# The opening of an FFT-and-MLP kernel: input ahead of the weights, most scratch rows written late, weights prepared inside the first steps

## The chip, the core and the metric

The kernel runs on one NeuronCore of a Trainium2 chip. The metric is the device time of one execution in microseconds (us). The core has five engines, each with its own queue that is worked off in order: TensorE (PE, matrix products; PEld is its loading of weights), VectorE (DVE), ScalarE (ACT), GpSimd (POOL) and SyncE (SP, here only an issuer of transfers). Transfers are issued by SP and by GpSimd, and all of them share the same 16 DMA engines.

## What is computed

A two-dimensional Fourier transform over sequence and channels, of which the real part is kept, and then a two-layer MLP with the hard-swish activation:

```python
X = np.fft.fft(x, axis=1)          # x: (8, 3008, 256)
X = np.fft.fft(X, axis=2).real
x = X.reshape(24064, 256)
h = x @ w_in                       # (256, 2048), float64 in memory
g = h * np.clip(h + 3.0, 0.0, 6.0) / 6.0
out = g @ w_out                    # (2048, 256), float64 in memory
```

## The kernel before

**Stages.** The eight sequences are worked in four pairs. The transform over 3008 = 47 x 64 positions has two stages. For stage 1, x is loaded in eight chunks per pair (`load_x`, L136: the rows themselves, L146, and their mirrored partners by an indirect transfer, L155, whose indices `IX` come with the constants `F`). A fold (`fold`, L160, five additions and subtractions) makes sums and differences of rows and mirrored rows; one matmul of 512 columns per half chunk with `F` (`stage1`, L214, L227) follows, and `evict_z` (L230) copies the result to the tile z and writes it to a scratch tensor `zd` in DRAM. Column 128 needs another treatment: `turn_column` (L251) writes it, with signs changed, to a second scratch tensor `zq` in 4-byte elements. `load_g` (L261) reads the scratch back, turned, in six groups per pair; `stage2` (L271, L284) multiplies a group with a table `T`, and `spread` (L290) spreads one row of its result over all partitions (`qn`). The transform over channels is not done at all: it is folded into w_in (`fold_w_in`, L566), which makes `W1`; one row of W1 is kept in another layout as `WN`, by way of DRAM (L580, `load_wn`).

**Main loop.** The MLP runs in 12 chunks per pair and 8 steps per chunk, 384 steps in all (`steps`, L742). In step s, `mlp1` (L324) is issued for step s + 2: four first-layer matmuls of 256 columns into two PSUM tiles u and v (L334), two operations on VectorE that add the row WN (L339), a sum and a difference (L349, L351), two relus on ScalarE (L376) and two gates on VectorE (L379) that give the tile a with four blocks. `combine` (L381) makes sums of these blocks on GpSimd (L393). `mlp2` (L395) multiplies seven blocks (Strassen's scheme in Winograd's form: seven products in place of eight) with seven combinations `G` of w_out (L403) and accumulates over the 8 steps; `finish` (L413) puts the seven results together on GpSimd, and `store` turns and writes them. A matmul in 32-bit floats shows as two records in the trace.

**Weights.** w_in and w_out come as 64-bit floats and are turned into 32-bit ones by hand, in 16 pieces of 512 KB (`PIECES`, L480; `load_w`, L485, issued by GpSimd). A piece takes, on ScalarE, the two parts of `exponent_a` (L509) and `exponent_c` (L518); on TensorE, `exponent_b` (L514, two matmuls that subtract 16-bit numbers); on VectorE, `mantissa` (L526, L527) and `join` (L535 or L542). Two finished pieces of w_in go to `fold_w_in` (L574, copies to W1 on ScalarE, L579), two of w_out to `mix_w_out` (L556), which makes the combinations G on VectorE (L561 to L564).

**Order.** The order on each engine is the program's order. In the opening, the loop over the chunks of pair 0 (L658) takes one chunk of x and one weight piece together; these chunks use shorter functions (`fold_first`, L184, three VectorE operations, and `stage1_first`, L194, four matmuls per half chunk) save the last one. Then come the load of g for group 0 and seven more pieces (L677), each with a filler product (`keep_awake`, L594) for TensorE's clock; after that stage 2 and `spread` of group 0 and the first two `mlp1`. The last piece is finished after step 1 (`after`, L698). What is done beside the steps of a pair (further stage-2 groups, and loading, folding and stage 1 of the next pair, nine steps per chunk, the fold on GpSimd) stands in `beside` (L700) with step numbers.

Of the kernel before, what the change touches and what calls it, by code (L numbers as in the profile page):

```python
# [51 lines left out]

PROD = ("P1", "P2", "-P4", "P5", "P7", "-P6", "P3")
# [3 lines left out]
def kernel(  # L57
# [51 lines left out]
    F = consts.tile([PR + 2, 5 * PZ + NP * NXC + 1], F32, name="F")  # L109
# [17 lines left out]
    def x_tile(pr, i):  # L127
        pool, tag = xpool, "x"
        if pr.p == 0 and 4 <= i < 13:
            pool, tag = ((apool, "a"), (cpool, "c"), (spool, "t"))[(i >= 8) + (i >= 11)]  # L130
        return pool.tile([PR + 2, XC, D], F32, tag=tag, name="xt")
# [8 lines left out]
    def load_forward(pr, c):  # L140
        xt = x_tile(pr, 2 * c)

        nr = PR + 2 if pr.p < NP - 1 else PR
        rows = x_pn[pr.p * PR:pr.p * PR + nr]
        n = XC if c < NXC - 1 else XC - 1
        nc.gpsimd.dma_start(out=xt[0:nr, 0:n, :], in_=rows[:, c * XC + 1:c * XC + 1 + n, :])  # L146
        if n < XC:
            nc.gpsimd.dma_start(out=xt[0:nr, n:XC, :], in_=rows[:, 0:1, :])
        pr.x[c] = xt

    def load_partners(pr, c):
        xr = x_tile(pr, 2 * c + 1)
# [31 lines left out]
    def fold_first(pr, c):  # L184
        xt, xr = pr.x[c][0:PR], pr.xr[c][0:PR]
        r = xr[:, ::-1, :]
        y = ypool.tile([PR, XC + 1, D], F32, tag="y", name="y")
        tt = nc.vector.tensor_tensor
        tt(y[:, 0:XC, 1:P], xt[:, :, D - 1:P:-1], r[:, :, 1:P], op=AL.add)
        tt(xt[:, :, 1:P], xt[:, :, 1:P], r[:, :, D - 1:P:-1], op=AL.add)  # L190
        tt(xt[:, :, 0:P + 1:P], xt[:, :, 0:P + 1:P], r[:, :, 0:P + 1:P], op=AL.add)
        pr.y[c] = y

    def stage1_first(pr, c, i):  # L194
        sl = slice(2 * i, 2 * i + 2)
        a, b = pr.x[c][0:PR, sl, :], pr.y[c][:, sl, 1:P]
        ps = bank([P, 2, D], "ps1")
        for k, (f, m, c0) in enumerate([(F[0:PR, 0:PZ], a[:, :, 0:P + 1], 0), (F[0:PR, 0:PZ], b, 1),
                                        (F[0:PR, 0:PZ], a[:, :, 1:P], P + 1), (FN[0:PR], b, P + 1)]):
            nc.tensor.matmul(ps[0:PZ, :, c0:c0 + m.shape[2]], f, m, start=(k == 0), stop=(k > 0),  # L200
                             skip_group_check=True)
        evict_z(pr, c, i, ps)
        if i == XC // 2 - 1:
            del pr.x[c], pr.xr[c]
# [9 lines left out]
    def stage1(pr, c, i):  # L214

        y = pr.y[c]
        ps = bank([P, 2, D], "ps1")
# [10 lines left out]
        evict_z(pr, c, i, ps)  # L228

    def evict_z(pr, c, i, ps):  # L230
        if i == 0:

            pool, tag = (gpool, "g") if pr.p == 0 and c % 3 == 2 else (zpool, "z")
            pr.z[c] = pool.tile([PZ, XC, D], F32, tag=tag, name="z")
            if c == 0:
                pr.zd = dpool.tile([2, NK1, 2, NS, D], F32, tag="zd", name="zd")
                pr.zq = dpool.tile([2, NK1, 2, NS], F32, tag="zq", name="zq")
        z = pr.z[c]
        nc.scalar.copy(z[:, 2 * i:2 * i + 2, :], ps[0:PZ])  # L239
        if i == XC // 2 - 1:  # L240
            nc.sync.dma_start(
                out=pr.zd[:].rearrange("b k c n d -> (b k c) n d")[:, c * XC:(c + 1) * XC, :],
                in_=z[:],
            )
            turn_column(pr, c, z)
            del pr.y[c], pr.z[c]

# [3 lines left out]
    def turn_column(pr, c, z):  # L251
        n = XC if c < NXC - 1 else XC - 1
        zc = zpool.tile([PZ, XC], F32, tag="zc", bufs=4, name="zc")
        nc.scalar.activation(zc[:, 0:n], z[:, 0:n, P], AF.Identity, scale=F[0:PZ, 5 * PZ + NP * NXC:])
        cs = slice(c * XC, c * XC + n)
        nc.sync.dma_start(out=pr.zq[:, :, ::-1, cs].rearrange("b k c n -> (b k) c n"), in_=zc[:, 0:n])
        if n < XC:
            nc.sync.dma_start(out=pr.zq[:, :, :, c * XC + n].rearrange("b k c -> (b k c)"), in_=z[:, n, P])


    def load_g(pr, gr):  # L261
        g = gpool.tile([P, 2 * KK, D + 1], F32, tag="g", name="g")
        ks = slice(gr * 2 * KK, (gr + 1) * 2 * KK)
        gb = [g[b * N2:(b + 1) * N2] for b in range(2)]
        for b in range(2):
            nc.sync.dma_start(out=gb[b][:, :, 0:D], in_=pr.zd[b].rearrange("k c n d -> (c n) k d")[:, ks, :])
        for b in range(2):
            nc.sync.dma_start(out=gb[b][:, :, D], in_=pr.zq[b].rearrange("k c n -> (c n) k")[:, ks])
# [36 lines left out]
    class Chunk:  # L305
# [3 lines left out]
        def __init__(self, pr, ck):  # L309
            self.pr, self.ck = pr, ck  # L310
            self.last = ck == NCK - 1
            self.final = self.last and pr.p == NP - 1
# [81 lines left out]

    def mlp2(ch, fc):  # L395
# [78 lines left out]
    FN = wpool.tile([PR + 2, PZ], F32, tag="FN", name="FN")  # L474
# [8 lines left out]
    raw, exs, fracs, w = {}, {}, {}, {}  # L483

    def load_w(j):  # L485
        kind, n, i = PIECES[j]
        st = wpool.tile([P, 2 * WB], I32, tag="st", bufs=4, name="st")
# [17 lines left out]
    def exponent_a(j):  # L505
        top = raw[j][:].bitcast(I16).rearrange("p (n four) -> p n four", four=4)[:, :, 3]
        for i in range(2):
            low = PM[:, j % 2, i].bitcast(U8).rearrange("p (n two) -> p n two", two=2)[:, :, 0]
            nc.scalar.activation(low, top, AF.Identity, bias=bias[:, i:i + 1], scale=(1 - 2 * i) / 16.0)  # L509

    def exponent_b(j):
        ex = ps_h.tile([P, WB], F32, tag="uv", name="ex")
        for i in range(2):
            nc.tensor.matmul(ex[:], E[:, i], PM[:, j % 2, i].bitcast(F16), start=(i == 0), stop=(i == 1))  # L514
        exs[j] = ex
# [4 lines left out]
    def mantissa(j):  # L520
# [3 lines left out]
        top = wpool.tile([P, WB], I32, tag="top", bufs=2, name="top")  # L524
# [5 lines left out]
    def join(j):  # L530
# [8 lines left out]
        b12 = wpool.tile([P, 2, P], F32, tag="b12", bufs=2, name="b12")[:] if i == 0 else None  # L539
        for h, g in enumerate((block(n, 0), b12) if i == 0 else (block(n, 1), block(n, 6))):  # L540
            f, e = (t.rearrange("p (c q h e) -> h p c q e", c=2, h=2, e=DH)[h] for t in (frac, ex))
            nc.vector.tensor_tensor(g.rearrange("p c (q e) -> p c q e", e=DH), f, e, op=AL.mult)  # L542
        if i == 0:
            w[PIECES[j]] = b12
# [4 lines left out]
    def use_pair(j):  # L549
        kind, n, _ = PIECES[2 * j]  # L550
        if kind == "in":
            fold_w_in(n)
        else:
            mix_w_out(n)

    def mix_w_out(j):  # L556

        b12 = w.pop(("out", j, 0))
        g = [block(j, i) for i in range(7)]
        tt = nc.vector.tensor_tensor  # L560
        tt(g[3], g[0], b12, op=AL.subtract)  # L561
        tt(g[5], g[6], g[3], op=AL.add)
        tt(g[2], g[5], g[1], op=AL.subtract)
        tt(g[4], g[6], b12, op=AL.subtract)  # L564

    def fold_w_in(n):  # L566

        cs = slice(n * WB, (n + 1) * WB)
        ws = [w.pop(("in", n, i)) for i in range(2)]
        sums = []  # L570
        for blk in range(2):
            ps = bank([P, WB], "wps")
            for i in range(2):
                nc.tensor.matmul(ps[:], C[:, i, blk * P:(blk + 1) * P], ws[i], start=(i == 0), stop=(i == 1))  # L574
            sums.append(ps)

        def copy():
            for blk in range(2):
                nc.scalar.copy(W1[:, blk, cs], sums[blk][:])  # L579
            nc.sync.dma_start(out=wn[n:n + 1], in_=W1[P - 1:P, 1, cs])  # L580

        copies.append(copy)


    def load_wn(n):
        nb = WB // P
        nc.sync.dma_start(out=WN[:, n * nb:(n + 1) * nb], in_=wn[n].rearrange("(j p) -> p j", p=P))
# [6 lines left out]
    def keep_awake(n):  # L594
        ps = ps_h.tile([P, 2 * TB], F32, tag="uv", name="awake")
        for i in range(n):
            nc.tensor.matmul(ps[:], ones[:], Z[:], start=True, stop=True)  # L597
# [4 lines left out]
    keep_awake(6)  # L602
    nc.sync.dma_start(out=F[:], in_=c_stage1)
# [4 lines left out]
    PM = wpool.tile([P, 2, 2, WB], I16, tag="PM", name="PM")  # L608
    nc.vector.memset(PM[:].rearrange("p j i n -> p (j i n)").bitcast(I32), 0x64006400)
    nc.vector.tensor_copy(IX[:], F[:, 5 * PZ:5 * PZ + NP * NXC])  # L610
    nc.scalar.mul(FN[:], F[:, 0:PZ], -1.0)
# [3 lines left out]
    nc.sync.dma_start(out=C[:], in_=dim[:, :, 0:D])  # L615
    E = wpool.tile([P, 2, P], F16, tag="E", name="E")
    nc.scalar.copy(E[:], CE[:])
    for b in range(2):
# [3 lines left out]
    wn = dpool.tile([NWI, WB], F32, tag="wn", bufs=1, name="wn")  # L622


    load_forward(first, 0)
    load_partners(first, 0)
    load_w(0)
    load_x(first, 1)
    load_w(1)
# [3 lines left out]
    pending, copies = [], []  # L633

    def on_scalar(j):
        for i in pending:
            exponent_c(i)
        if j is not None:
            exponent_a(j)
# [3 lines left out]
    def on_vector(j):  # L643
        if j is not None:
            mantissa(j)
        for i in pending:
            join(i)

    def on_tensor(j):
        if j is not None:  # L650
            exponent_b(j)
        done = pending.pop() if pending else 0
        if done % 2:
            use_pair(done // 2)
        if j is not None:
            pending.append(j)

    for c in range(NXC):  # L658
        if c + 2 < NXC:
            load_x(first, c + 2)  # L660
        load_w(c + 2)
        if c < NXC - 1:
            fold_first(first, c)
        else:
            for part in range(2):
                fold(first, c, part, nc.vector)
        on_scalar(c)
        on_vector(c)
        for i in range(XC // 2):
# [181 lines left out]
```

## Time and profile before

| | us |
|---|---|
| median of 3 runs (lowest, highest) | 1979.77 (1979.23, 1982.34) |
| the profiled execution, its time | 1980.04 |
| its span in the profile | 1978.3 |
| first stage-2 matmul (L284) | 77.4 |
| first second-layer product (L403), step 0 | 92.06 |
| TensorE busy in 0 to 100 us | 86.57 |
| TensorE busy in 300 to 400 us | 100.00 |
| ScalarE busy in 0 to 100 us | 60.08 |
| VectorE busy in 0 to 100 us | 59.99 |

In the profile, L12 means line 12 of the kernel before. A row of a group gives line, engine and operation, the tiles written and read, shapes and count, then busy time and the mean of one in nanoseconds, and then how long the engine stood idle ahead of these instructions and for whom. A row of waits gives who waited for whom: total, how often, longest. The chain of waits goes back from the last instruction, at each step to what released it; its rows are start, duration, what. PEclk, and the clock column of the stretches, is the TensorE clock granted, as a part of full speed.

### The profile page before, as it was taken

The page shows a single profiled execution, that of the slowest core. Times are in us where ns is not written, and L with a number is a line of the kernel's source. Part 1 is how long each engine was busy: PE and PEld are TensorE (multiplying, and loading weights), DVE is VectorE, ACT ScalarE, POOL GpSimd, SP SyncE. Part 2 cuts the span into 40 slices and gives each one's busy share as a digit, 9 for nine tenths or more (in the row PEclk, how much of TensorE's full clock was granted, in tenths as well). Part 3 has the DMA queues.
Part 4 walks back from the last instruction along what each step waited for, and adds up shares of the span by engine and source line. Part 5 has one row for each costly group of instructions (what it writes and reads, how often), then busy time and mean ns, then how long its engine had stood idle before and what let it go on. Part 6 is the DMA issues. An engine that isn't in the chain of part 4 may idle for free.

```text
span 1978.3 us, 27746 instructions
## 1 busy us (share of the span) xinstructions
PE 1949.1 (99%) x9178; PEld 1685.4 (85%) x9178; DVE 1433.5 (72%) x2775; ACT 687.9 (35%) x1164; POOL 1414.2 (71%) x1604
## 2 busy tenths in 40 slices
PE   8899999999999999999999999999999999999998
PEld 5588888888998888888898888888889888888887
DVE  5677767776787776776777776777678777777776
ACT  6533333333333333333333333333333333333332
POOL 4277778786687787777768877778667667666765
PEclk9999999999999999999999999999999999999999
DMA  9502211111111111221111221212110101111000
GB/s 307 136 26 61 51 41 46 49 49 35 27 36 51 41 49 48 54 59 24 36 32 30 63 55 44 56 41 54 37 22 23 30 14 25 26 24 28 17 20 20
DMA packets 149701, 93.31 MB, mean 47 GB/s; under 512 B 121739, under 2 KB 135055, under 8 KB 149558
## 3 DMA queue, kind: packets, MB, share of 16 engines
q1 hardware_dynamic: 139294, 57.86, 12.2%
q0 software_dynamic: 9472, 33.49, 5.9%
q8 instruction: 72, 1.18, 0.2%
q14 instruction: 71, 0.58, 0.1%
q10 hardware_dynamic: 792, 0.20, 0.0%
HBM read 54.19 MB, written 37.33 MB: 46 GB/s over the span
## 4 chain that ended last, share of the span: by engine, by line
PE 93%; DVE 2%; ACT 1%; issue 0%; DMA 0%; SPq 0%; DVEq 0%; ACTq 0%
PE acc L403 56%; PE v L334 16%; PE u L334 16%; PE ps L284 2%; PE ps L227 2%; DVE a L379 1%; DVE s L339 1%; ACT t L376 0%; ACT PM L509 0%; DVE o L461 0%; PE wps L574 0%; DVE u L360 0%; PE ps L224 0%; PE ex L514 0%; PE awake L597 0%
## 5 line engine op out<-in xcount | busy, mean ns | idle before, releaser
L393 POOL TENSOR_TENSOR c<-a 128x512 f32<-128x512 f32 (+1 forms) x383 | 478.2, 1248 | 431.4 <-PE acc L403 369.3
L403 PE MATMUL acc<-c,G 128*128 128x256 f32 (+1 forms) x3072 | 712.0, 375 | 0.0
L376 ACT ACTIVATE t<-u,half 128x512 f32<-128x512 f32 (+1 forms) x384 | 261.0, 680 | 1100.5 <-DVE u L349 1018.7
L403 PEld LDWEIGHTS acc<-c,G 128*128 128x128 f32 x3072 | 577.5, 190 | 72.7
L339 DVE SCALAR_TENSOR_TENSOR s<-qn,WN,u 128x256 f32<-128x256 f32 (+1 forms) x768 | 330.0, 471 | 354.3 <-PE u L334 354.0
L403 PE MATMUL acc<-a,G 128*128 128x256 f32 (+1 forms) x2304 | 551.2, 375 | 0.0
L403 PEld LDWEIGHTS acc<-a,G 128*128 128x128 f32 x2304 | 433.8, 190 | 55.9
L334 PE MATMUL v<-q,W 127*128 127x256 f32 (+1 forms) x1536 | 390.1, 376 | 4.4 <-DVE a L379 4.4
L334 PE MATMUL u<-q,W 128*128 128x256 f32 (+1 forms) x1536 | 388.3, 375 | 2.4 <-DVE a L379 2.1
L379 DVE SCALAR_TENSOR_TENSOR a<-t,u 128x512 f32<-128x512 f32 (+2 forms) x448 | 263.7, 600 | 104.9 <-ACT t L376 102.1
L334 PEld LDWEIGHTS u<-q,W 128*128 128x128 f32 x1536 | 285.7, 190 | 58.2 <-issue 14.8
L334 PEld LDWEIGHTS v<-q,W 127*128 127x128 f32 x1536 | 288.7, 190 | 45.1 <-DVE a L379 4.1
L393 POOL TENSOR_TENSOR c<-c,a 128x256 f32<-128x256 f32 (+1 forms) x383 | 274.8, 717 | 30.0
L393 POOL TENSOR_TENSOR c<-a,c 128x256 f32<-128x256 f32 (+1 forms) x383 | 274.6, 717 | 30.1
L349 DVE TENSOR_TENSOR u<-s,v 128x512 f32<-128x512 f32 x352 | 245.0, 696 | 37.7 <-PE v L334 0.8
L379 DVE SCALAR_TENSOR_TENSOR a<-t,v 128x512 f32<-128x512 f32 (+1 forms) x480 | 263.2, 564 | 0.0
L376 ACT ACTIVATE t<-v,half 128x512 f32<-128x512 f32 (+1 forms) x384 | 260.5, 678 | 0.0
L351 DVE TENSOR_TENSOR v<-v,s 128x512 f32<-128x512 f32 x352 | 243.7, 692 | 0.0
L393 POOL TENSOR_TENSOR r<-w,e 128x256 f32<-128x256 f32 (+1 forms) x94 | 90.8, 987 | 3.7
L411 ACT ACTIVATE e<-acc 128x512 f32<-128x512 f32 (+2 forms) x190 | 86.3, 545 | 3.4 <-PE acc L403 3.3
L461 DVE STREAM_TRANSPOSE o<-r 128x256 f32<-128x256 f32 (+1 forms) x192 | 72.5, 414 | 0.2
L239 ACT COPY z<-ps 96x512 f32<-96x512 f32 x64 | 37.2, 582 | 83.7 <-PE ps L227 65.2
(91 smaller groups left out, 780.2 us busy)
## 6 DMA issues: line engine op xcount, KB each, us to landing
out_dram<-o SPq DMA_DIRECT2D x746, 32.0 KB
zd<-z SPq DMA_DIRECT2D x32, 384.0 KB
g<-zd SPq DMA_DIRECT2D x48, 256.0 KB
xt<-in_x_dram POOLq DMA_DIRECT2D x21, 384.0 KB, 4.1
qn<-qd SPq DMA_DIRECT2D x19, 256.0 KB
st<-in_moe_w_in_dram POOLq DMA_DIRECT2D x8, 512.0 KB, 9.1
st<-in_moe_w_out_dram POOLq DMA_DIRECT2D x8, 512.0 KB, 5.1
xt<-in_x_dram POOLq DMA_DIRECT2D x7, 376.0 KB, 3.9
```

The source lines that it names most:

```text
L227: nc.tensor.matmul(ps[0:PZ], F[0:PR, 0:PZ], y[:, 2 * i:2 * i + 2, :], start=True, stop=True)
L284: nc.tensor.matmul(ps[:, blk, u * P:n].rearrange("p (b k) -> p b k", b=2), g[:, kk, blk * (P + 1):blk * (P + 1) + P], T[:, :, gr, blk, kk, ...
L334: nc.tensor.matmul(ps[:, i, 0:nq], W1[r, blk, f * P:(f + 1) * P], q[r, blk, of:of + nq], start=True, stop=True)
L339: nc.vector.scalar_tensor_tensor(s[:, i, 0:nq], qn[:, of:of + nq], WN[:, f:f + 1], u[:, i, 0:nq], op0=AL.mult, op1=AL.add)
L349: nc.vector.tensor_tensor(u[:], s[:], v[:], op=AL.add)
L351: nc.vector.tensor_tensor(v[:], v[:], s[:], op=AL.subtract)
L376: nc.scalar.activation(t, h, AF.Relu, bias=half[:], scale=scale)
L379: nc.vector.scalar_tensor_tensor(dst, t, 1.0, h, op0=AL.min, op1=AL.mult)
L393: (eng or nc.gpsimd).tensor_tensor(out, in0, in1, op=AL.add)
L403: nc.tensor.matmul(ch.acc[i // 2][:, i % 2, 0:ch.n], G[:, i, fc, :], mv, start=(fc == 0 and i % 2 == 0), stop=(fc == NF - 1), skip_group_c ...
L411: nc.scalar.mul(ch.e[:, k:i + 1, 0:ch.n], ch.acc[i // 2][:, 0:i + 1 - k, 0:ch.n], 1.0 / WS)
L461: nc.vector.transpose(o[:, 0:n // DH, h], ch.r[:, m, h, 0:n].rearrange("p (j i) -> p j i", i=DH))
```

## The change

The change rewrites the opening, up to step 9 of the 384 steps:

- In the loop over pair 0's chunks there are no weights any more. The last chunk comes first (`ORDER`), x is loaded three chunks ahead, and all eight chunks take the full fold and the plain `stage1`. The index columns and the constants come in two transfers (`FI`, `F`). Weight pieces 0 to 3 are loaded behind the last chunks of x; 4 to 7 only after a small GpSimd copy (`seen`) that waits for g of group 0; pieces 8 to 15 each when an earlier one has been read (`NEXT`).
- For pair 0, column 128 is made by a small matmul of its own (`turned_column`, with a sixth table in `F`) and stored as a 257th column, so that `zq` is not used there. The scratch has the groups outermost. At first only the 16 rows of group 0 are written; the 80 others wait in their tiles (`later`) and are written in steps 0 to 3, two chunks a step. The load of group 1 stands at step 5, its stage 2 at steps 7 and 11; the next pair's chunks begin at step 8 and follow every eight steps.
- Chunk 0 of pair 0 multiplies the four blocks of w_out as they are (`mlp2_first`): four matmuls of 512 columns a step, eight block products, with no `combine` and no `finish`. `mlp1` runs one step ahead there, two from step 8 on.
- A weight piece is worked in a unit: exponent_b of piece j, then exponent_a and mantissa of piece j + 1, then exponent_c and join of j. Pieces 0 to 5 come before step 0, the ten others in steps 0 to 4 (`DUE`). Odd pieces from 5 on subtract on VectorE in place of the matmul. `fold_w_in` works on half quarters; WN is made by small matmuls in the opening and by transfers from W1 later. `mix_w_out` moves to GpSimd, in steps 4, 5, 6 and 9.

```diff
+    ORDER = [NXC - 1] + list(range(NXC - 1))
+    def x_tile(pr, c):
+        pool, tag = (spool, "t") if pr.p == 0 and ORDER.index(c) % 3 == 2 else (xpool, "x")
...
+    def turned_column(pr, c, y):
+        n = XC if c < NXC - 1 else XC - 1
+        pt = ps_h.tile([P, 2 * TB], F32, tag="uv", name="pt")
+        nc.tensor.matmul(pt[0:PZ, 0:n], F[0:PR, 5 * PZ:6 * PZ], y[:, 0:n, P], start=True, stop=True)
...
+            else:
+                n0 = PZ // NG
+                nc.sync.dma_start(out=zd[0:n0], in_=z[0:n0])
+                later.append((zd[n0:], z[n0:]))
...
+    def mlp2_first(ch, fc):
+        a = ch.a.pop(fc)
+        for h in range(2):
+            if fc == 0:
+                ch.acc[h] = ps_a.tile([P, 2, TB], F32, tag="acc", name="acc")
+            for f in range(2):
+                nc.tensor.matmul(ch.acc[h][:], G[:, (B11, B12, B21, B22)[2 * f + h], fc, :], a[:, :, f],
+                                 start=(fc == 0 and f == 0), stop=(fc == NF - 1 and f == 1))
+        if fc == NF - 1:
+            ch.r = epool.tile([P, 2, 2, TB], F32, tag="r", name="r")
+            for h in range(2):
+                for m in range(2):
+                    nc.scalar.mul(ch.r[:, m, h], ch.acc[h][:, m], (1 - 2 * m) / WS)
...
+    STRAIGHT = (0, 1, 8, 9, 14, 15)
+    NEXT = {0: 8, 1: 9, 4: 10, 5: 11, 6: 12, 7: 13, 8: 14, 9: 15}
...
     def exponent_b(j):
+        pm = [PM[j % 2][:, i].bitcast(F16) for i in range(2)]
+        if j >= 4 and j % 2:
+            exs[j] = wpool.tile([P, WB], F32, tag="ex", bufs=2, name="ex")
+            nc.vector.tensor_tensor(exs[j][:], pm[0], pm[1], op=AL.subtract)
+            return
...
     def mix_w_out(j):
-        tt = nc.vector.tensor_tensor
+        tt = nc.gpsimd.tensor_tensor
...
+    def fold_w_in(n, h):
+        nb = WB // 2
+        ps = bank([P, 2, nb], "wps") if starting[0] else spare[len(copies) % 2]
...
+    def head(j):
+        exponent_a(j)
+        mantissa(j)
+        if j in NEXT:
+            load_w(NEXT[j])
+    def tail(j):
+        exponent_c(j)
+        join(j)
+        if j % 2 and PIECES[j][0] == "in":
+            folds.extend((PIECES[j][1], h) for h in range(2))
+    def unit(j):
+        exponent_b(j)
+        if j + 1 < len(PIECES):
+            head(j + 1)
+        tail(j)
...
+    for c in ORDER[0:3]:
+        load_x(first, c)
+    for k, c in enumerate(ORDER):
+        for part in range(2):
+            fold(first, c, part, nc.vector)
+        for i in range(XC // 2):
+            stage1(first, c, i)
+        keep_awake(1)
+        if k + 3 < NXC:
+            load_x(first, ORDER[k + 3])
         else:
+            for j in (2, 3) if k == 5 else ():
+                load_w(j)
+        if k == 4:
+            load_w(0)
+            load_w(1)
             load_t(0)
...
     load_g(first, 0)
+    nc.gpsimd.tensor_copy(seen[:], first.g[0][:, 0, 0:1])
+    for j in range(4, 8):
+        load_w(j)
+    head(0)
+    exponent_b(0)
+    keep_awake(1)
+    head(1)
+    tail(0)
+    exponent_b(1)
+    keep_awake(1)
+    head(2)
+    tail(1)
+    exponent_b(2)
+    fold_w_in(*folds.pop(0))
+    head(3)
+    tail(2)
+    exponent_b(3)
+    copy_all()
+    tail(3)
     for i in range(2):
         stage2(first, 0, i)
     spread(first, 0)
+    fold_w_in(*folds.pop(1))
+    copy_all()
...
+    DUE = [((), (6,)), ((7,), (8, 9)), ((10, 11), (12,)), ((13,), (14,)), ((15,), ())] + [((), ())] * 3
+    head(4)
     mlp1(*chunk(0))
+    exponent_b(4)
+    head(5)
+    tail(4)
+    fold_all()
+    unit(5)
...
+        if s < NF:
+            mlp1(*chunk(s + 1))
+            fold_all()
+            for j in DUE[s][0]:
+                unit(j)
+            if s == NF - 1:
+                combine(*chunk(NF))
+            mlp2_first(*chunk(s))
+            for dst, src in later[2 * s:2 * s + 2]:
+                nc.sync.dma_start(out=dst, in_=src)
+            for j in DUE[s][1]:
+                unit(j)
+            if 4 <= s < NF - 1:
+                mix_w_out(s - 4)
+            if s == NF - 1:
+                mlp1(*chunk(NF + 1))
+        else:
...
```

## The prediction, made before the changed kernel was run

> **What bounds the kernel now.** I read the page first (busy shares), then the chain of waits from 40 to 140 us, then the busy time by stretches, then the waits of the first 135 us and the groups of instructions up to 92 us.
>
> ```profile
> PE 1949.1 (99%) x9178; PEld 1685.4 (85%) x9178; DVE 1433.5 (72%) x2775; ACT 687.9 (35%) x1164; POOL 1414.2 (71%) x1604
> ...
> PE 93%; DVE 2%; ACT 1%; issue 0%; DMA 0%; SPq 0%; DVEq 0%; ACTq 0%
> ```
>
> From the first product on TensorE is the bound: in the chain the second-layer products of one step take 3.02 us, the first-layer ones 0.86 + 0.86, 4.75 us a step, with nothing between. The change touches none of that after step 9, so what it is worth is read in the opening alone.
>
> ```profile
> 92.06 3.53 PE acc L403 x14
> ...
> 129.34 3.02 PE acc L403 x14
> ```
>
> The first line is step 0: no product of the second layer runs before 92.06. The second is step 7; it ends at 132.4, and this is my yardstick. By then TensorE has also done the first-layer products of steps 8 and 9 and both halves of group 1 of stage 2; everything behind is the same work in both kernels.
>
> ```profile
> 20.00:30.00 10.00, 10.00 (x40) 6.37 (x39) 5.47 (x10) 6.33 (x12) 4.33 (x6) 1.00 1.03 352
> ...
> 60.00:70.00 10.00, 8.86 (x23) 3.52 (x22) 4.28 (x9) 6.69 (x12) 1.42 (x2) 1.00 0.85 221
> ```
>
> Columns after the stretch: its length, PE, PEld, DVE, ACT, POOL busy, the clock, DMA share, GB/s. Up to 50 us the transfers are full (1.03 of the queues' time, 352 GB/s): x, 16 weight pieces of 512 KB and the whole scratch compete. From 56 to 80 no engine is full; ScalarE and TensorE hand each other weight pieces.
>
> ```profile
> DVE y L189 <- DMA xt<-in_x_dram,IX: 16.6, 7, 5.5
> ...
> POOL st L493 <- ACT PM L509: 19.0, 7, 4.9
> ...
> SPq L301 <- ACT q L287: 47.7, 1, 47.7
> ```
>
> The fold of x waits 16.6 us for x, the later weight loads wait 19.0 for ScalarE to free their buffers, and the sixteen pieces are all done (bar the last) before stage 2 runs at 77.4, though its input was asked for at 57.4.
>
> ```profile
> L509 ACT ACTIVATE PM<-st,bias 128x512 uint8<-128x512 int16 x32 | 22.6, 758 | 1.6 <-DVE xt L191 0.8 <-DMA st<-in_moe_w_in_dram 0.7
> ...
> L527 DVE SCALAR_TENSOR_TENSOR top<-st,top 128x512 f32<-128x512 uint32 x16 | 11.1, 696 | 0.6
> ...
> L518 ACT ACTIVATE ex<-ex 128x512 int32<-128x512 f32 x15 | 8.7, 580 | 3.4 <-PE ex L514 3.3
> ...
> L526 DVE TENSOR_SCALAR top<-st 128x512 int32<-128x512 int32 x16 | 6.9, 429 | 3.4 <-DMA st<-in_moe_w_in_dram 2.3 <-DMA st<-in_moe_w_out_dram 0.8
> L535 DVE TENSOR_TENSOR wi<-top,ex 128x512 f32<-128x512 f32 x8 | 5.5, 684 | 6.2 <-ACT ex L518 6.2
> ```
>
> These are the prices of a weight piece ("unit"): ScalarE 2 x 0.758 + 0.580 = 2.1 us, VectorE 0.43 + 0.70 + 0.68 = 1.8.
>
> **What the Trainium skill says.** "DMA: Bandwidth & Descriptors", "Anatomy of one DMA", gives about 2 us of fixed time per transfer; the trace agrees: F, issued at 0.75, is there at 3.46. "TensorE: Matmul & The Clock Gate", "What's actually happening", says that an idle window of 3.4 us halves the clock; the trace has a granted clock of 0.50 from 50 to 54 us, after a wait for the fold of 2.87 us, so it agrees roughly. "SBUF — State Buffer", "SBUF: two separate sides", says that a VectorE operation with two SBUF inputs and a GpSimd operation take turns at one port; the mixing of w_out agrees: 0.42 us each at 45 to 76 us, 0.83 to 1.48 at 101 to 105 us beside GpSimd.
>
> **The x phase, part by part.** *x ahead of the weights.* Loads are issued three chunks ahead into six buffers; no weight goes between them until five chunks are folded. The index column comes in its own small transfer, perhaps 0.4 us earlier than F's 3.46; the partners were issued at 3.94 and there at 9.11, so the first fold starts near 8.4. *The fold* is now the full one for all eight chunks: L166 to L180 took 3.0 us for the last chunk in the trace, and 4 x 0.61 + 0.17 = 2.6 for an ordinary one, against 1.4 for the three operations of `fold_first`: +10 us of VectorE in all, which lie beside x's arrival (0.77 MB at the 287 GB/s of 6 to 8 us is 2.7 us a chunk). A load goes out when the fold three chunks back is done, 1.8 us of issue and 4.2 of landing (4.91 to 9.11); with the fold 8.7 us per three chunks, 2.9 each. I take 3.0: eight folds end at 32. TensorE per chunk falls from 16 matmul records of 0.21 us to 4 of 0.43 plus the turned column (a few columns, 0.1 to 0.3, like the 0.11 steps of L284) and one keep-awake of 0.86: about 2.8, just inside the pace. ScalarE's extra column copy (0.30, the price of the L254 row it replaces) costs nothing.
>
> *Late scratch rows.* Only 16 of 96 rows go out at once (66 KB of 395), and the 4-byte transfers of zq go for this pair. Last z on ScalarE at 34, in scratch at 36, g asked for over 1.3 us (57.40 to 58.69), there at 40. What a load of g lasts no row shows: at least the 2 us of any transfer, at most 20 (asked for at 57.4, used at 77.4). I take 3 since DMA is then nearly empty. The 80 rows left (2.6 MB) follow in steps 0 to 3; the load of group 1 then has until step 7, some 40 us, at a DMA load well under 300 GB/s: hidden. Were it 10 us late, TensorE would stand 10 us at stage 2 in step 7.
>
> **Weights until step 0.** Units 0 to 3 begin on ScalarE at 34: 4 x 2.1 and about 0.5 lost per exchange with TensorE (the period seen is 2.36, 71.64 to 74.00) give 44. Stage 2, spread and their copies took 3.5 us (77.4 to 80.9), then the fold of W for two halves, 1.7 us each (8 matmuls of L574 took 3.43) with copies of 0.58: the first products at 49 and 1.7 us long. VectorE's share of one step is 0.87 + 0.7 + 0.69 + 2 x 0.69 with ScalarE's relu between, 82.03 to 85.80: 3.75 us; done at 54. Then units 4 and 5 must be finished before the first second-layer product: 4.5 us. **Step 0 multiplies at 58.5**, against 92.06.
>
> **Steps 0 to 7.** *Eight products in place of seven:* four matmuls of 512 columns, 8 x 0.43 = 3.46 against 3.02, +0.43 a step, 3.5 us. GpSimd's combine (1.27 + 2 x 0.73) and the finish go for this chunk; they were hidden, so nothing. *The units inside the steps:* VectorE has seven more step shares, 26.3, and units 6 to 15: five even ones at 1.85, four odd at 2.25 (with the subtraction in place of the matmul, not in the trace; from 0.3, as it is 16-bit, to 0.68 as L535; I take 0.4), the last 1.15: 19.4. Together 58.5 + 45.7 = 104.2. TensorE alone has 27.7 + 13.8 + 6.9 (the folds of two quarters in step 2) + 2.2 + 1.9 = 52.5, ending at 111: two queues almost equally full, so neither hides the other. In step 2 they meet: ScalarE's copies of W stand behind the relus of step 3, the folds wait for the two spare banks, and units 10 and 11 stand behind both and ahead of the product of step 2; I make this 5 us of VectorE idle, 0 to 8. Ten handovers at 0.47 add 4.7. Behind the last VectorE share follow the product of step 7, the first layer of step 9 and half of stage 2: 3.5 + 1.7 + 0.9. Sum: 104.2 + 5 + 4.7 + 6.1 = **120**.
>
> *Mixing of w_out on GpSimd:* 4 x 0.72 per block in steps 4, 5, 6 and 9, in time GpSimd has free; VectorE's two-SBUF-input operations may wait beside it, up to 3 us in all, which I leave in the range. The next pair's loads at 8 steps in place of 9 add 10% to GpSimd in pair 0, whose busy time is 7.8 of 10 us there: cover suffices, and beyond that nothing is late since the chain holds TensorE only.
>
> **Sum.** 132.4 - 120 = 12.4 us less. Span 1978.3 - 12.4 = 1965.9; the profiled execution had 1980.04, 1.7 above its span, so 1967.6; the median of the runs shown, 1979.77, is 0.3 lower. Forecast **1968**, own range 1960 to 1975.
>
> **The rivals.**
> *It flows.* No stop in step 2, handovers hidden: 120 - 10 = 110, set by TensorE's 111; 1958. For it: VectorE has room ahead of every product. Against: the waits of 56 to 80 us, where the same exchange never reached full use.
> *Late g.* If g takes 10 us more, ScalarE and VectorE go on with units until 44 and 5 to 6 us are lost: 1974. For it: DMA share 1.10 at 60 to 62 while g was loaded. Against: weights shared the queues then.
> *Break-even.* Units cost about 1 us more each than summed (12 from unit 4 on): gain gone, 1978 to 1982.
> *Slower: units in series.* Place: ScalarE's queue in steps 0 to 4. Each unit's exponent stands behind relus that wait for VectorE, its matmul behind a product on TensorE, so that a unit costs its whole round: 1.5 + 0.47 + 0.43 + 0.58 + 0.3 + 0.75 = 4.0 against the 2.4 counted. 12 x 1.6 = 20 us: 1988. It decides from 1.4 us a unit (16.4 us, the gain and 0.2%). For it: in the trace unit 15 and its mixing made step 2 to 3 7.4 us (102.06 to 109.44) in place of 4.75. Against: part of that was mixing, now on GpSimd, and units are one ahead.
>
> **How the numbers follow.** Forecast 0.50, flows 0.20, late g 0.07, break-even 0.08, series 0.15. About 0.2%, 4 us, is what the measurement can tell from no change. Faster 0.77, same 0.08, slower 0.15. The range 1955 to 1984 leaves the series case and the best end of the flowing one outside, just 2 in 10.
>
> **What would show it.** Last fold at 32; first stage-2 matmul at 44 to 46; first 512-column product at 58.5; step 7 ending near 120; a chunk-0 step above 7 us in steps 1 to 3 and 5.2 from step 6. Wrong it would be if GpSimd waits for g beyond 45, if TensorE idles in step 7 for g, if the clock stays at half through the folds of step 2 (3.4 us more), or if later steps leave 4.75.

## The result and the profile after

No change: 1979.41 us median against 1979.50 in the same runs, ratio 0.9999 (95% interval 0.9982 to 1.0016). Run again later, beside the experiments, the changed kernel had 0.9995 (0.9988 to 1.0003). Predicted was 1968, 0.6% faster. The span went from 1978.3 to 1977.4 us.

The busy shares and the chain of waits of the changed kernel, from its page:

```profile
PE 1943.2 (98%) x9110; PEld 1670.8 (84%) x9110; DVE 1442.8 (73%) x2780; ACT 687.5 (35%) x1165; POOL 1399.4 (71%) x1592
...
PE 92%; DVE 4%; ACT 2%; DMA 1%; issue 1%; POOL 0%; SPq 0%; DVEq 0%; ACTq 0%
```

TensorE has 6 us less to do and holds 92% of the chain in place of 93: what it saved it now waits. VectorE's and ScalarE's parts of the chain have doubled. The chain of waits in order of time shows where (start, duration, what; in the changed kernel L406 is `mlp2_first`, L422 `mlp2`, L591 `fold_w_in`):

```profile
58.45 1.14 PE acc L406 x2
...
79.39 6.19 PE spare L591 x16
...
90.80 4.54 PE acc L406 x6
...
122.40 3.44 PE acc L406 x8
...
131.10 3.02 PE acc L422 x14
```

The first line is the product of step 0: at 58.45 us, against 92.06 before. The opening did gain its 33.6 us. The last is the product of step 8: 131.10, against 134.96 before, where the chain of the kernel before has

```profile
126.72 0.89 PE ps L284 x8
...
132.37 0.86 PE ps L227 x2
...
134.96 3.02 PE acc L403 x14
```

So step 0 to step 8 lasts 72.65 us where it lasted 42.9 before, and 3.9 us of the lead are left. Of these, 1.75 are only postponed: half of group 1 of stage 2 (0.89) and a piece of the next pair's stage 1 (0.86), which the kernel before has behind it by then. About 2 us are real, and 0.9 are in the span.

Where the 30 us go shows in the stretches around step 2 (length, then PE, PEld, DVE, ACT, POOL busy, clock, DMA share, GB/s):

```profile
73.00:78.00 5.00, 1.09 (x6) 0.61 (x4) 4.86 (x7) 0.59 (x2) 3.24 (x4) 0.96 0.39 134
78.00:83.00 5.00, 3.61 (x9) 2.90 (x10) 2.46 (x5) 1.82 (x4) 0.00 (x0) 0.50 0.05 0
83.00:88.00 5.00, 3.00 (x11) 2.02 (x9) 0.01 (x1) 2.98 (x6) 0.00 (x0) 0.86 0.04 0
```

From 73 to 78 us VectorE is full and TensorE has 1.1 us to do; from 83 to 88 VectorE does nothing at all. No transfer is the reason: DMA is at 0.04. The waits of the first 140 us name the releasers (L602 is the copy of a fold to W1, L532 exponent_a, L545 exponent_c, L568 the join of a w_out piece, L170 the first operation of the fold of x, L379 a relu, `seen` the copy that waits for g):

```profile
POOL seen L701 <- DMA g<-zd: 15.1, 1, 15.1
DVE G L568 <- ACT ex L545: 12.3, 4, 7.3
...
DVE xt L170 <- DMA xt<-in_x_dram,IX: 6.7, 6, 4.0
...
PE spare L591 <- ACT W L602: 5.3, 1, 5.3
```

The wait of the fold of x for its transfer fell from 16.6 to 6.7 us, as meant. In its place VectorE waits 12.3 us for ScalarE, 7.3 in one piece, and TensorE 5.3 us for a copy. The timeline of these engines around that piece (start, duration, engine, line; in brackets how long the engine stood idle ahead of it, and for whom):

```profile
70.47 3.62 PE L591 MATMUL spare<-wi,C 128*128 128x256 f32 x16
...
78.17 0.69 ACT L379 ACTIVATE t<-v,half 128x512 f32<-128x512 f32 x1
78.76 1.06 ACT L602 COPY W<-spare 128x512 f32<-128x512 f32 x2
...
79.39 6.18 PE L591 MATMUL spare<-wi,C 128*128 128x256 f32 x16 [5.30 <-ACT W L602]
...
85.60 0.59 ACT L602 COPY W<-spare 128x512 f32<-128x512 f32 x1 [1.81 <-PE spare L591]
86.08 1.38 ACT L532 ACTIVATE PM<-st,bias 128x512 uint8<-128x512 int16 x2
87.37 0.59 ACT L545 ACTIVATE ex<-ex 128x512 int32<-128x512 f32 x1
87.99 0.75 DVE L568 TENSOR_TENSOR G<-top,ex 128x256 f32<-128x256 f32 x2 [7.34 <-ACT ex L545]
88.47 1.12 PE L406 MATMUL acc<-a,G 128*128 128x512 f32 x2 [2.47 <-DVE G L568]
...
96.42 0.75 DVE L568 TENSOR_TENSOR G<-top,ex 128x256 f32<-128x256 f32 x2 [3.87 <-ACT ex L545]
```

Read it from the top. The folds of w_in's second quarter are done by 74 us. Their copies stand on ScalarE behind the two relus of step 3, which come when VectorE has caught up, at 78. Only then are the two spare banks free for the fourth quarter's folds, and those run at half clock, 6.2 us in place of 3.6, after TensorE has stood for 5.3. Behind them stands unit 10's exponent matmul, on ScalarE unit 10's exponent_c behind the last copy and the exponent of unit 11, and behind that VectorE's join. Only with units 10 and 11 joined can step 2 multiply. The last line is a second wait of the same kind, 3.9 us: the join of unit 12, behind that product.

### The profile page after: what moved, and what is told of

Its sections match the earlier page's. It is cut to its first block, busy times and chain, and to the rows that moved or that the text cites. A ratio compares the mean times of both kernels' runs of the same rounds, so it can differ in the third digit from the quotient of the medians.

```text
span 1977.4 us, 27573 instructions
## 1 busy us (share of the span) xinstructions
PE 1943.2 (98%) x9110; PEld 1670.8 (84%) x9110; DVE 1442.8 (73%) x2780; ACT 687.5 (35%) x1165; POOL 1399.4 (71%) x1592
## 4 chain that ended last, share of the span: by engine, by line
PE 92%; DVE 4%; ACT 2%; DMA 1%; issue 1%; POOL 0%; SPq 0%; DVEq 0%; ACTq 0%
PE acc L422 55%; PE v L337 16%; PE u L337 16%; PE ps L213 2%; PE ps L286 2%; DVE a L382 1%; DVE s L342 1%; DMA xt<-in_x_dram,IX 1%; PE acc L406 1%; ACT t L379 1%; ACT PM L532 0%; DVE o L480 0%; PE spare L591 0%; DVE u L363 0%; DVE u L352 0%
## 5 line engine op out<-in xcount | busy, mean ns | idle before, releaser
L396 POOL TENSOR_TENSOR c<-a 128x512 f32<-128x512 f32 (+1 forms) x375 | 468.3, 1249 | 407.9 <-PE acc L422 332.8
L422 PE MATMUL acc<-c,G 128*128 128x256 f32 (+1 forms) x3008 | 696.9, 374 | 0.0
L379 ACT ACTIVATE t<-u,half 128x512 f32<-128x512 f32 (+1 forms) x384 | 260.8, 679 | 1104.5 <-DVE u L352 1025.3
L422 PEld LDWEIGHTS acc<-c,G 128*128 128x128 f32 x3008 | 565.4, 190 | 71.1
L422 PE MATMUL acc<-a,G 128*128 128x256 f32 (+1 forms) x2256 | 538.8, 374 | 0.0
L422 PEld LDWEIGHTS acc<-a,G 128*128 128x128 f32 x2256 | 423.4, 190 | 54.9
L396 POOL TENSOR_TENSOR c<-a,c 128x256 f32<-128x256 f32 (+1 forms) x375 | 268.6, 716 | 29.4
L396 POOL TENSOR_TENSOR c<-c,a 128x256 f32<-128x256 f32 (+1 forms) x375 | 268.3, 716 | 29.4
L379 ACT ACTIVATE t<-v,half 128x512 f32<-128x512 f32 (+1 forms) x384 | 260.7, 679 | 1.0 <-PE acc L422 0.8
L213 PE MATMUL ps<-y,F 94*96 94x512 f32 x120 | 61.3, 601 | 5.2 <-ACT q L289 5.2
```

The costliest lines, as they stand in the source:

```text
L213: nc.tensor.matmul(ps[0:PZ], F[0:PR, 0:PZ], y[:, 2 * i:2 * i + 2, :], start=True, stop=True)
L379: nc.scalar.activation(t, h, AF.Relu, bias=half[:], scale=scale)
L396: (eng or nc.gpsimd).tensor_tensor(out, in0, in1, op=AL.add)
L422: nc.tensor.matmul(ch.acc[i // 2][:, i % 2, 0:ch.n], G[:, i, fc, :], mv, start=(fc == 0 and i % 2 == 0), stop=(fc == NF - 1), skip_group_c ...
```

## The experiments

Three theories. **A, a stop:** the order of folds, copies and units in step 2 makes three queues wait for each other in turn. **B, sheer work:** VectorE and TensorE are full over steps 0 to 7, and a stop that is avoided is a wait elsewhere. **C, side effects:** the half clock of TensorE, or GpSimd's mixing of w_out, which runs beside the units. The measure is the time from the product of step 0 to that of step 8 in the chain ("between" in the table), as the opening itself varies from profile to profile. Behind step 8 all these kernels but one (the mixing behind the combines) need 1846.2 to 1846.6 us to the end of the span, so what is gained between is kept. Two profiles of one kernel differ by 1.0 us (changed kernel) and by 1.7 (three reorderings) in this measure; a smaller difference needs a place in the profile that shows it.

| run | step 0 | step 8 | between | ratio to the kernel before (95%) |
|---|---|---|---|---|
| changed kernel | 58.45 | 131.10 | 72.65 | 0.9999 (0.9982 to 1.0016) |
| changed, again | 63.20 | 136.85 | 73.65 | 0.9995 (0.9988 to 1.0003) |
| folds moved, unit 12 ahead of the product | 60.40 | 123.87 | 63.47 | 0.9944 (0.9927 to 0.9960) |
| folds moved alone | 63.94 | 130.17 | 66.23 | 0.9957 (0.9942 to 0.9973) |
| mixing behind the combines | 60.92 | 129.92 | 69.00 | 0.9988 (0.9982 to 0.9995) |
| mixing gated | 59.80 | 128.29 | 68.49 | 0.9976 (0.9968 to 0.9985) |
| all units ahead of step 0 | 85.05 | 131.44 | 46.39 | 0.9984 (0.9977 to 0.9990) |
| filler products | 60.48 | 131.66 | 71.18 | 0.9984 (0.9976 to 0.9991) |
| step 9 between the halves | 59.54 | 130.67 | 71.13 | 0.9984 (0.9977 to 0.9990) |
| three reorderings | 58.33 | 116.86 | 58.53 | 0.9929 (0.9917 to 0.9942) |
| three reorderings, again | 59.78 | 120.03 | 60.25 | 0.9926 (0.9907 to 0.9945) |

**The stop in step 2 taken away.** The same work in another order:

```diff
             mlp1(*chunk(s + 1))
-            fold_all()
             for j in DUE[s][0]:
                 unit(j)
+                if j == 11:
+                    fold_all()
...
             for j in DUE[s][1]:
                 unit(j)
+            if s == 1:
+                fold_w_in(*folds.pop(0))
+                fold_w_in(*folds.pop(0))
+                copy_all()
```

and `DUE` for step 2 is `((10, 11, 12), ())`.

> The changed kernel with another order in steps 1 and 2: the two folds of w_in's second quarter and their copies stand at the end of step 1, those of the fourth quarter behind units 10 and 11, and unit 12 ahead of the product of step 2. No work is added or taken away. Theory A (a stop: in step 2 the folds wait for copies that stand on ScalarE behind the relus of step 3, and units 10 and 11 stand behind the folds): VectorE's stop of 7.3 us at 80.6 goes, the first operation of the first layer of step 4 on VectorE starts near 90 in place of 97.1, the first product of step 8 near 124 in place of 131.1, time 1979.4 - 7 = 1972. Theory B (sheer work: VectorE and TensorE are full over steps 0 to 7, a stop avoided is a wait elsewhere): step 8 starts at 129 to 131, time 1978 to 1980. Theory C (clock: the half clock from 78 on is what costs): about 3 us, 1976.

63.47 us, 9.2 less, and 0.9944. The timeline of VectorE in this run, at the place of the stop:

```profile
82.15 0.69 DVE L554 SCALAR_TENSOR_TENSOR top<-st,top 128x512 f32<-128x512 uint32 x1
82.90 0.75 DVE L568 TENSOR_TENSOR G<-top,ex 128x256 f32<-128x256 f32 x2
83.57 0.68 DVE L538 TENSOR_TENSOR ex<-PM 128x512 f32<-128x512 f16 x1
```

The join (L568) follows the mantissa ahead of it (L554) with no wait, where 7.34 us stood between them. Theory A holds, and B falls for this stop: no wait of that size took its place. That it is 9.2 and not 7.3 is in part the clock (the last six records of step 2's product took 2.84 us here, 4.54 in the changed kernel) and in part unit 12. The next run keeps unit 12 behind the product (`((10, 11), (12,))`):

> As the run with the folds moved, but unit 12 stays behind the product of step 2, so that its exponent matmul stands behind that product. From step 0 to the first product of step 8 the changed kernel took 72.65 us, the run with both moved 63.47. If the stop has two parts, folds and copies ahead of unit 10, and unit 12 behind the product, this one lies between, near 66.5 us (VectorE waits about 3 us for the exponent of unit 12), ratio near 0.996. If the folds alone were the stop, 63.5 to 64 us and ratio 0.994.

66.23, as expected. So moving the folds is worth about 6.4 us and unit 12 another 2.8, each from one pair of profiles; the ratios of the two runs alone can't be told apart. The waits of this run from 70 to 131 us:

```profile
DVE G L568 <- ACT ex L545: 5.5, 2, 4.8
```

That is the second part of the stop: VectorE's join of unit 12 waits for an exponent whose matmul stands on TensorE's queue behind the whole product of step 2, whose last six records took 5.44 us here.

**All units ahead of step 0**, as the kernel before has them: `DUE = [((), ())] * 8`, and behind `unit(5)` a loop over units 6 to 15 with `fold_all()` from 9 on.

> The changed kernel with all ten units of steps 0 to 4 put ahead of step 0, as the kernel before has them. No work is added or taken away. Theory B and the series rival (a unit inside the steps costs as much time as one alone): step 0 multiplies at 58.5 + 10 x 2.2 + four copies 2.4 = 83, eight steps at 5.2 us follow, step 8 starts at 124 to 128 and the time is 1973 to 1977, no worse than the changed kernel. Theory A with real overlap (only the one stop costs, the rest of the units is hidden beside products): step 8 starts at 133 or later, time 1981 or more.

Its chain of waits:

```profile
85.05 3.90 PE acc L406 x8
90.87 3.44 PE acc L406 x8
...
131.44 3.02 PE acc L422 x14
```

Steps without units last 5.2 us and step 8 starts at 131.4, between the two forecasts (124 to 128, or 133 and later). The ratio is no worse than the changed kernel's, so nothing is lost against it. Here ten units cost about 85.05 - 60.6 = 24.5 us (60.6 is where step 0 stood in the three other runs of that series), in the changed kernel's steps 72.65 - 46.39 = 26.3. As ordered, a unit inside the steps is no cheaper than one alone. With folds and unit 12 moved it is 63.47 - 46.39 = 17.1: overlap can be had, and step 2 had used it up.

**The clock.** Five products of 512 columns that nobody uses, between the two pairs of folds (`fold_all(5)` in the steps):

```diff
             if len(copies) == 2:
                 copy_all()
+                if filler and folds:
+                    ps = bank([P, 2 * TB], "fill")
+                    for i in range(filler):
+                        nc.tensor.matmul(ps[:], ones[:], C[:].rearrange("p h d -> p (h d)"), start=True, stop=True)
```

> The changed kernel with five extra products of 512 columns, used by nobody, between the two pairs of folds in step 2, where TensorE waits 5.3 us for the copies; they take 4.3 us. Theory C (the clock): the granted clock stays 1.0 at 78 to 88, the last folds last 3.5 us in place of 6.2, the product of step 2 3.5 in place of 4.5, step 8 starts 3 us earlier, time 1976. Theories A and B: the clock is better, and the folds shorter, but the units still wait for copies on ScalarE; at most 2.7 us of it reach step 8, 1977 to 1979.

71.18, 1.5 us less, half of what theory C asks and within what A and B allow. The chain:

```profile
81.42 3.73 PE spare L591 x16
...
90.37 5.49 PE acc L406 x6
```

The folds are 2.5 us shorter, at a granted clock of 1.00. But then TensorE stands as before for units 10 and 11, and the six records of the product of step 2 take 5.49 us in place of 4.54, at a clock of 0.50 from 90 to 95 us. So about 1 us of the 2.5 only moves to the work behind the next hole. As the clock did not stay up, the run does not show what the slow clock costs in all.

**The mixing.** Two ways to take it from beside the units. First behind the combines of steps 7 to 10:

> The changed kernel with the mixing of w_out on GpSimd moved behind the combines of steps 7 to 10, so that GpSimd does none of it while weight units are worked. No work is added or taken away. If GpSimd's mixing beside VectorE's two-SBUF-input operations costs what the trace shows (L553 1.27, L554 1.10, L562 1.21 at 72 to 76 in place of 0.42, 0.69, 0.69, and about 1.3 at 101 to 105), the step 8 product starts 3 us earlier, at 128, time 1976.5. If another wait is behind it, the operations are short and step 8 still starts at 131, time 1979. Worse by some 2 us if the mixing is then late for steps 8 to 10.

69.00, as the port theory has it, but the span is 1979.0: 2.8 us are lost again behind step 8. Its chain, where the product of step 12 waits for a combine that stands in step 11:

```profile
151.13 1.04 POOL xt L171
152.17 1.23 POOL c L396
...
155.05 0.70 PE acc L422 x2
```

There GpSimd, with four mixings and the next pair's fold ahead of its combine, is itself the last to come. Then with a gate, a copy of one column that waits for the last unit, so that mixing runs in steps 5 to 7:

```diff
+            if s == 4:
+                nc.gpsimd.tensor_copy(seen[:], G[:, B22, NF - 1, 0:1])
             if 4 <= s < NF - 1:
                 mix_w_out(s - 4)
```

> The changed kernel with one tiny GpSimd copy ahead of the mixing that waits for the last weight unit, so that mixing runs beside steps 5 to 7 and not beside the units, and is done before the combines of chunk 1 (where the earlier run with late mixing lost 2.8 us). Port theory: step 0 to step 8 lasts 69 us (3.7 less, as in the earlier run) and nothing is given back, ratio near 0.998 or 1976 where the kernel before is 1979.5. Rival (GpSimd is needed in steps 5 to 7 after all, or the wait ends elsewhere): 71 to 73 us, no change against the changed kernel.

68.49 and nothing given back: the span is 1846.2 us past the start of step 8, and 1846.3 in the changed kernel. In the changed kernel the program puts mixing in steps 4 to 6, but GpSimd had nothing ahead of it and began at 72.60 (L577), during the units of step 1. The timeline of VectorE and GpSimd there:

```profile
72.35 1.27 DVE L553 TENSOR_SCALAR top<-st 128x512 int32<-128x512 int32 x1
72.60 0.73 POOL L577 TENSOR_TENSOR G<-G 128x256 f32<-128x256 f32 x1
...
73.66 1.10 DVE L554 SCALAR_TENSOR_TENSOR top<-st,top 128x512 f32<-128x512 uint32 x1
74.69 1.21 DVE L562 TENSOR_TENSOR wi<-top,ex 128x512 f32<-128x512 f32 x1
```

And with the gate, the same three operations:

```profile
73.71 0.42 DVE L553 TENSOR_SCALAR top<-st 128x512 int32<-128x512 int32 x1
74.17 0.69 DVE L554 SCALAR_TENSOR_TENSOR top<-st,top 128x512 f32<-128x512 uint32 x1
74.78 0.68 DVE L562 TENSOR_TENSOR wi<-top,ex 128x512 f32<-128x512 f32 x1
```

1.8 us in these three alone. The Trainium skill says in "SBUF — State Buffer", section "SBUF: two separate sides", that VectorE instructions with two SBUF inputs, or in a mode that uses two ports, share a pair of ports with GpSimd's: the one that starts first holds it for its whole length and the other waits in full. The trace agrees that both engines lose: the four mixing operations took 0.73 to 1.05 us beside the units, and 0.72 to 0.73 with the gate. That the wait is in full it does not show.

**From one step ahead to two.** `mlp2_first` takes a function that it calls between its halves; in step 7 this is `mlp1` of step 9.

> The changed kernel with the first layer of step 9 put between the two halves of the product of step 7, in place of behind it, so that going from one step ahead to two does not set two first layers side by side. Theory: between the product of step 7 and that of step 8 TensorE waits 2.4 us for gates on VectorE; half a product, 1.7 us, moves into that wait: step 8 starts 1.7 us earlier, step 0 to step 8 near 71 us, time about 1978. Rival: VectorE sets the end of that stretch and nothing moves, 72.6.

71.13, 1.5 us less. The chain from the product of step 7, now in two halves, to that of step 8 (L408 is `mlp2_first` here, L424 `mlp2`):

```profile
123.46 1.72 PE acc L408 x4
...
126.99 1.72 PE acc L408 x4
...
130.67 3.02 PE acc L424 x14
```

In the changed kernel the first layers of steps 9 and 10 stand side by side, and the second waits for the gates of the first. Neither the ratio of this run, 0.9984 against the changed kernel's 0.9995, nor 1.5 us in 72 would tell this alone. The place does: from the product of step 7 to that of step 8 it is 8.7 us in the eight profiles without this edit (122.40 to 131.10 in the changed kernel) and 7.2 in the three with it.

**All three**, and then all three again beside the unaltered changed kernel on one chip:

> All three together: folds and unit 12 moved in steps 1 and 2, the gate ahead of the mixing, the first layer of step 9 between the halves. If the three stops are separate, 63.5 - 3 - 1.7 = 59 us from step 0 to step 8, 1.5% or so of the opening's loss back: ratio about 0.9925, 1965 where the kernel before is 1979.5. If TensorE's own work (52.5 us) or VectorE's 45.7 and more sets a floor, 60 to 62 us and 0.9935.

> The changed kernel unaltered, on the chip and in the rounds of the next run, to have both against the same runs of the kernel before. From the profiles: step 0 to step 8 again 72.6 us; ratio 0.997 to 1.000, no change that can be told. If the chips of the experiments favour the changed kernel by themselves, its ratio here is below 0.997 and the gains of the experiments are smaller than they look.

> The kernel with all three reorderings again, beside the unaltered changed kernel: step 0 to step 8 58.5 us, ratio 0.993, so 0.5% to 0.7% under the changed kernel. If the earlier gain came from a lucky opening (its step 0 was at 58.3, others had 59.5 to 63.9), ratio 0.995 to 0.996 here.

58.53 and 60.25 us, ratios 0.9929 and 0.9926; in the second, 1968.29 us where the changed kernel had 1980.59 and the kernel before 1981.50. So the gain is not that of a lucky opening. The gains nearly add: 9.2 + 4.2 + 1.5 = 14.9, measured 14.1 and 13.4. The 1.7 us between the two profiles are in the folds at the end of step 1: 3.29 us at a clock of 1.00 in the first, 4.97 at 0.70 in the second. The chain of the first of the two runs:

```profile
58.33 1.14 PE acc L408 x2
...
81.99 2.84 PE acc L408 x6
...
113.18 1.72 PE acc L408 x4
...
116.86 3.02 PE acc L424 x14
```

Step 2's product is at 82 in place of 90.8. From 70 to 120 us TensorE is busy 48.1 of 50 us there and VectorE 42.5: now TensorE is near full, and on it the floor that theory B spoke of is close.

## Why the prediction was wrong

**Right: the way to step 0.** The last fold was to end at 32 and ended at 32.7; stage 2 was to start at 44 to 46 and did at 43.9; step 0 was to multiply at 58.5 and did at 58.45. That it fits so closely is luck: in the other profiles with the same opening step 0 stands at 58.3 to 63.9. g landed later than I put it (asked for by 39.9, there at 43.5, not 40), but that is what the units cover. Behind step 0 no engine waited for a transfer in the profile of the changed kernel; group 1's stage 2 in step 7 waited for nothing.

**Wrong: the sum of steps 0 to 7.** By my terms the first layer of step 9 ends at 120, so that the product of step 8, behind the first layer of step 10 (1.7), starts at 121.7, 63.2 us after step 0. It took 72.65, 9.4 more. The terms that failed:

- *"In step 2 they meet ... I make this 5 us of VectorE idle, 0 to 8."* The place and the mechanism were right: copies behind relus, two spare banks, units behind both. The size was 7.3 + 3.9 = 11.2. I followed the queues up to the join of unit 11 and stopped. That the clock may stay at half through the folds I named as a sign of being wrong, but left out of the sum; and I didn't count that unit 12's exponent stands behind the product, which is late itself. Taking both away gave 9.2.
- *Mixing: "up to 3 us in all, which I leave in the range."* It cost 4.2 (72.65 to 68.49; 3.7 in the other run without it), and had to be in the sum. I took the steps in which the program puts it for the time at which it runs; GpSimd, with nothing ahead of it in its queue, ran it in step 1.
- *No term at all* for the change from one step ahead to two: 1.5.
- *The 16-bit subtraction*, 0.4 of 0.3 to 0.68: it took 0.69 like the 32-bit one, five times 0.3 = 1.5 more. That is its size; no run shows what of it reached step 8.

These make 6.2 + 4.2 + 1.5 + 1.5 = 13.4 where 9.4 were missing; the 4.7 us for ten handovers, an allowance, was too much by about the rest. That last part is argued, not measured.

*The yardstick* was not level either: the kernel before has both halves of group 1's stage 2 behind it at 132.4, my sum for the changed kernel had one. That is 0.9 us of the 12.4 forecast that was never to be won.

**The rivals.** What came true in time is what I gave 0.08, break-even. Its reason, units about 1 us dearer than summed, fits only in the sum (9.4 us over ten units): the excess sits in a few places, and mixing and the step ahead are no unit's cost. My slower rival named the right place, ScalarE's queue, and its reason, exponents behind relus and matmuls behind products; it overstated how many units are caught, two or three and not twelve. "It flows" would be 53.2 us from step 0 to step 8; the three reorderings, at 58.5 and 60.3, stand about midway between it and the forecast.

**The last microsecond.** At step 8 the changed kernel is 2.1 us ahead in work, at the end 0.9. TensorE's waits from 136 to 500 us, the kernel before first and then the changed one, are 1.5 us apart, which accounts for it (waiter, releaser, total, times, longest):

```profile
PE ps L227 <- ACT q L287: 1.2, 2, 0.7
PE ps L213 <- ACT q L289: 2.7, 4, 0.7
```

Stage 1 of the next pair waits for a copy of stage 2, four times in place of two. With eight steps a chunk, half of stage 1 of every second chunk falls into a step that has a stage 2 (steps 19, 35, 51 and 67); with nine steps a chunk this happens twice (35 and 71). This is read from the program and the traces; no run changes it.

## What to carry to other kernels

A lead won before a loop is not yet a gain (here 0.9 of 33.6 us reached the end): add up, for the steps behind it, every instruction on every in-order queue between two points where all are level, and follow a stop to its second and third victim. Moved work that shares a queue with a tight loop should have no instruction ahead of one that the loop waits for; here the same work in another order was worth 9 us. Work put on an idle engine may run long before the step in which the program has it (here in step 1 in place of 4), so if it slows a busy engine, gate it.

## What was unexpected of the hardware

- A subtraction of 16-bit numbers in SBUF, 128 x 512, took 0.69 us on VectorE, the same as the 32-bit one; its result is 32 bits wide here. The single-input operation L553 took 1.27 us in place of 0.42 beside GpSimd, three times as long, where the two-input ones took 1.6 to 1.8 times.
- After a wait of 5.3 us TensorE's granted clock stood at 0.50 from 78 to 83 us, and 16 matmul records took 6.19 us that take 3.6 at full clock. Filler ahead of them took 2.5 us off, and 1 us of that came back on the product behind the next wait.
- The transfers of x differ from run to run. The fold of the sixth chunk waited 1.27 us in one profile of the changed kernel and 2.95 in the other; step 0 lies between 58.3 and 63.9 in profiles whose openings are the same. This is more than most of the effects studied here, and the reason to measure them between two points of one profile.
